# A row load three stores forward in SyncE's order, and three of eight buckets' records loaded from GpSimd's queue

## The chip, the cores and the metric

The kernel runs on one core of a Trainium2 chip. Five engines work side by side, each on its own instruction queue: TensorE (PE; its weight loads are PEld), VectorE (DVE), ScalarE (ACT), GpSimd (POOL) and SyncE (SP), which here issues DMAs and nothing else. GpSimd issues DMAs too. The metric is the device time of one launch in microseconds, the median of several runs.

## What is computed

Block-causal attention (blocks of 64) over 8 batches, 8 heads, 576 positions and head size 64 gives a matrix x of 4608 tokens by 512; a noisy top-2 router then sends each token through two of eight experts:

```python
scores = np.where(mask, scale * np.matmul(q, k.transpose(0, 1, 3, 2)), -1000000000.0)
attn = np.exp(scores - np.max(scores, axis=-1, keepdims=True))
attn = attn / (np.sum(attn, axis=-1, keepdims=True) + 1e-09)
x = np.matmul(attn, v)                                  # as (4608, 512)
noisy_logits = x @ w_gate + np.log1p(np.exp(x @ w_noise)) * noise
top2 = np.argpartition(-noisy_logits, 2, axis=1)[:, :2]
...
h = np.maximum(x[mask] @ w1[e], 0.0)                    # 512 -> 1024
out[mask] += top2_w[mask, k, None] * (h @ w2[e])        # 1024 -> 512
```

## The kernel before

**Stages.** Attention runs first, in four groups of two batches; each group is routed as soon as it is done. GpSimd scatters every token's row of x, with a record of 16 bytes (its two row numbers, a weight, the token's number), into a table in HBM (`xd`, one per half of the tokens). The table has eight buckets of 640 rows per half, one per expert. From about 125 us on TensorE works through 16 buckets in order: 0 to 7 are the first half's experts 0 to 7, 8 to 15 the second half's. A bucket is 640 rows through the expert's two layers: layer 1 (L1017) in two pieces of 320 rows by eight steps, each followed by a relu on ScalarE (L1023), then layer 2 (L1033) in five tiles of 128 rows.

**What a bucket needs.** Its rows: `load_x` (L934), one transposing DMA of 640 rows by 512 from `xd`, issued by SyncE into one of three buffers that take turns (`xg0`, `xg1` and `xT`); in the planner's table it is `LX5.0`, `LX6.0` and so on. Its weights: `load_w` (L910 for layer 1, L912 for layer 2), four DMAs of 512 KB that GpSimd issues and that convert from float32 to bfloat16. They land in memory that attention has left: bucket 5's in `vt`, bucket 6's in `qT` and `kT`, bucket 7's in `esc`.

**What a bucket leaves.** For the first half ScalarE copies each layer-2 tile out (`keep_row`, L1042, `Y.b.c` for tile c of bucket b) into one of ten buffers that take turns: `y0` to `y3`, `zero` and five tiles of `xr0`. SyncE then stores the tile to `yd` in HBM (`store_row`, L1049, `YS.b.c`, 128 KB). A buffer can be written again when its store has landed, ten tiles later: `Y.5.2`, `Y.5.3` and `Y.5.4` go where `Y.3.2`, `Y.3.3` and `Y.3.4` were. GpSimd later gathers rows from `yd` (L1056); VectorE adds and ScalarE scales them (L1040, L1069, L1091), and the sums are stored or scattered (L1075, L1103).

**The records.** `load_rec` (L973 to L976) reads the second half's records, 16 bytes each, into `rc`; `read_rec` (L984 to L1000) makes of them on VectorE the weights and row numbers that bucket 8 and all after it use.

**What sets the order.** A planner (`Plan`) simulates the engines with made-up costs and gives each step a due time; of the steps that could run on a free engine it takes the one due first. The order that comes out of it is fixed in the program: nothing is decided on the chip. `due` is thus a number that sorts, in the planner's time, not in the chip's. The row loads of buckets 2 to 15 are due 12 us ahead of the bucket:

```python
pl.add(f"LX{b}.0", {"SP": 0.3}, lambda x, b=b: load_x(b),
       deps=rows_of([2 * half, 2 * half + 1]), due=d0 - 12., take=[("xg", ("xg", b))],
       dma=2.5, packet=22, hold=True, seq="xg")
```

SyncE's DMAs take eight counters (`DMAHW0` to `DMAHW7`) in turn, so each DMA first waits until the eighth one before it has landed; GpSimd's do the same with `DMASW0` to `DMASW7`.

Of the kernel before, what the change touches and what calls it, by code (L numbers as in the profile page):

```python
# [11 lines left out]
I32 = mybir.dt.int32  # L12
# [200 lines left out]
def kernel(  # L213
# [12 lines left out]
    nc = tc.nc  # L226

    B, H, S, D = q.shape
    N, Dm = out.shape
    E = moe_w_gate.shape[1]  # L230
    F = moe_w1.shape[2]
    assert Dm == H * D and N == B * S
    P = 128
# [7 lines left out]
    CAP = 640  # L241
# [4 lines left out]
    OVB = E * CAP  # L246
    XR = OVB + 2 * TH * P
    DR = Dm + 8
# [12 lines left out]
    xd = [nc.dram_tensor(f"xd{i}", (XR, DR), BF16, kind="Internal").ap() for i in range(NH)]  # L261
# [58 lines left out]
    rc = low.tile([P, E, CT, 4], I32, name="rc")  # L320
# [91 lines left out]
    for g in range(NG):  # L412
        for ch in (4, 0, 1, 2, 3):
            for nm in "qk":
                pl.add(f"L{nm}{g}.{ch}", {"POOL": 0.58 if ch == 4 else 0.74}, lambda e, g=g, nm=nm, ch=ch: load_qk(g, nm, ch),
                       due=due_u(g, first_u[ch]) - (18.,18.,18.,22.)[g] + (0.1 if nm == "k" else 0) - (3 if ch == 4 else 0),
                       take=[("r" + nm, ("raw", g, nm, ch))], dma=0.7 if ch == 4 else 1.41, packet=88)
        for i in range(6):
            pl.add(f"V{g}.{i}", {"POOL": 1.18 if i < 4 else 0.7}, lambda e, g=g, i=i: load_v(g, i),
                   due=due_u(g, 6) - (8. if g else 16.) + i * 0.2, rel=0.0 if g < 1 else due_u(g, 0) - 8.,  # L420
                   take=[("vt", ("vt", g))] if i == 0 else [], deps=[f"V{g}.0"] if i else [],
# [55 lines left out]
    for g in range(NG):  # L477
        for nm in "qk":
            for ch in ("4B", 0, 1, 2, 3, "4A"):
# [4 lines left out]
                else:  # L484
                    need, u, lh = [f"L{nm}{g}.{ch}"], first_u[ch], last_h[ch]
                due = due_u(g, u) - 4 + (0.1 if nm == "k" else 0)
# [4 lines left out]
                       take=[("bk", ("tp", g, nm, ch), 1 if g else 0)], free=fr, lat=0.25)  # L491
# [4 lines left out]
                if ch == 0:  # L496
                    pl.add(f"CW{nm}{g}", {"DVE": 0.12}, lambda e, g=g, nm=nm: wrap(g, nm, e),
                           deps=[f"T{nm}{g}.0"] + ([s_name(g - 1, 7)] if g else []), due=due + 0.6, lat=0.15)
                pl.add(f"C{nm}{g}.{ch}", on,
                       lambda e, g=g, nm=nm, ch=ch: turned(g, nm, ch, e), deps=[f"T{nm}{g}.{ch}"] + prev,  # L500
                       due=due + 0.5, free=[("tp", g, nm, ch)], lat=0.15)
# [460 lines left out]
    def rows_of(gs):  # L962
        return [f"D{g}.{j}" for g in gs for j in range(2 * TG)]

    def rows_landed(ins, half, gs):
        own = [i for g in gs for i in scat[g]]
        apart(ins, f"scat{half}", own)
        for i in own:
            tc.add_manual_dep(ins.ins, i.name, SYNC_DEP, reason="rows landed")
        member(ins, f"rows{half}")  # L970
        return ins

    def load_rec():  # L973
        ins = nc.sync.dma_start(out=rc.rearrange("p e c w -> p (e c) w"),
                                in_=xd[1].bitcast(I32)[0:OVB, Dm // 2:DR // 2].rearrange("(c p) w -> p c w", p=P))
        return rows_landed(ins, 1, [2, 3])  # L976

    def read_rec():
        f = [rc[:, :, :, i].bitcast(I32 if i == 3 else F32) for i in range(4)]
# [130 lines left out]
    for b, i in ORDER:  # L1110
# [3 lines left out]
        if b < EARLY:  # L1114
            for c in range(c0 // P, (c0 + n) // P):
                pl.add(f"LX{b}.{c}", {"SP": 0.4}, lambda x, b=b, c=c: load_tile(b, c),
                       deps=rows_of(groups(b, c // 2)), due=d0 - 8 + c * 0.2, take=[("y", ("xl", b, c))], dma=0.4, packet=47)
                pl.add(f"XT{b}.{c}", {"PE": 0.23}, lambda x, b=b, c=c: turn_tile(b, c), mode="128*128", deps=[f"LX{b}.{c}"],
                       due=d0 - 3, take=[("bk", ("xp", b, c), 1)], free=[("xl", b, c)], lat=0.25)
                pl.add(f"XX{b}.{c}", {"DVE": 0.36, "ACT": 0.6}, lambda x, b=b, c=c: tile_turned(b, c, x),  # L1120
                       deps=[f"XT{b}.{c}"], due=d0 - 2, free=[("xp", b, c)], lat=0.2,
                       take=[("xg", ("xg", b))] if c == 0 else [])
                if c:
                    pl.ops[f"XX{b}.{c}"].deps.append(f"XX{b}.0")
        elif i == 0:
            pl.add(f"LX{b}.0", {"SP": 0.3}, lambda x, b=b: load_x(b),
                   deps=rows_of([2 * half, 2 * half + 1]), due=d0 - 12., take=[("xg", ("xg", b))],
                   dma=2.5, packet=22, hold=True, seq="xg")
        for st in range(FB // nb):
            d1 = d0 + st * nb * 0.55 * n / NW  # L1130
# [320 lines left out]
```

## Time and profile before

| | |
|---|---|
| median of 3 runs | 459.71 us (459.61 to 460.6) |
| the profiled execution | 462.31 us |
| its span, first to last instruction | 460.5 us |
| TensorE busy | 400.1 us (87%) |
| ScalarE busy | 256.0 us (56%) |
| GpSimd busy | 260.1 us (56%) |
| VectorE busy | 162.8 us (35%) |
| DMA queue q0, GpSimd's | 69856 packets, 52.37 MB, 67.3% of 16 engines' span |
| DMA queue q1, SyncE's | 58160 packets, 27.14 MB, 28.3% |

Busy times overlap; their sum says nothing. What counts is where TensorE, the busiest, stands still, and what it then waits for. The profile splits the span into 40 slices of 11.5 us and shows each engine's busy tenths in them; its waits name, for each idle stretch, what ended it; its timeline lists instructions with the time they start, how long they take and, in brackets, how long the engine was idle before them. A SyncE row is an issue: how long SyncE was held by it, not how long the transfer took.

### The profile page before, as it was taken

The page shows a single profiled execution, that of the slowest core. Times are in us where ns is not written, and L with a number is a line of the kernel's source. Part 1 is how long each engine was busy: PE and PEld are TensorE (multiplying, and loading weights), DVE is VectorE, ACT ScalarE, POOL GpSimd, SP SyncE. Part 2 cuts the span into 40 slices and gives each one's busy share as a digit, 9 for nine tenths or more (in the row PEclk, how much of TensorE's full clock was granted, in tenths as well). Part 3 has the DMA queues.
Part 4 walks back from the last instruction along what each step waited for, and adds up shares of the span by engine and source line. Part 5 has one row for each costly group of instructions (what it writes and reads, how often), then busy time and mean ns, then how long its engine had stood idle before and what let it go on. Part 6 is the DMA issues. An engine that isn't in the chain of part 4 may idle for free. (4 is left out here: it accounts for less than half of the span.)

```text
span 460.5 us, 10885 instructions
## 1 busy us (share of the span) xinstructions
PE 400.1 (87%) x4384; PEld 255.7 (56%) x4384; DVE 162.8 (35%) x451; ACT 256.0 (56%) x447; POOL 260.1 (56%) x293
## 2 busy tenths in 40 slices
PE   3899779869697999999899499999998998999950
PEld 3667666657456776555555165565554554655620
DVE  3768698877617510000000020023322423332320
ACT  2898687957791544745554154555554554655410
POOL 8756447877785775672120002433757777777760
PEclk9999999998999999999999799999999999999995
DMA  8999993999999799999999995758688477555430
GB/s 126 189 218 199 193 187 107 130 204 182 233 163 248 172 217 210 276 236 153 193 220 168 215 154 133 133 128 207 115 172 180 139 182 184 181 176 172 146 129 1
DMA packets 128073, 80.26 MB, mean 174 GB/s; under 512 B 85696, under 2 KB 115981, under 8 KB 128016
## 3 DMA queue, kind: packets, MB, share of 16 engines
q0 software_dynamic: 69856, 52.37, 67.3%
q1 hardware_dynamic: 58160, 27.14, 28.3%
q8 instruction: 36, 0.59, 0.5%
q14 instruction: 21, 0.17, 0.1%
HBM read 72.74 MB, written 35.17 MB: 234 GB/s over the span
## 5 line engine op out<-in xcount | busy, mean ns | idle before, releaser
L551 ACT ACTIVATE esc<-sc 128x1024 bf16<-128x1024 f32 x96 | 92.9, 1028 | 20.5 <-PE sc L532 20.0
L1033 PEld LDWEIGHTS <-h 128*128 128x128 bf16 x640 | 62.2, 98 | 72.7 <-issue 7.6
L790 POOL DMA_INDIRECT xd<-xr,slots x72 | 72.0, 1001 | 37.6 <-issue 17.3
L1023 ACT ACTIVATE h<-sc 128x320 bf16<-128x320 f32 (+1 forms) x120 | 49.6, 444 | 47.2 <-PE sc L1017 30.4
L1056 POOL DMA_INDIRECT xr<-yd,slots x36 | 36.8, 1021 | 66.5 <-DMA yd<-zero 44.8
L1023 ACT ACTIVATE h<-bk 128x320 bf16<-128x320 f32 (+1 forms) x124 | 55.7, 456 | 17.2 <-PE bk L1017 12.6
L1017 PEld LDWEIGHTS <-w 128*128 128x128 bf16 x448 | 40.8, 98 | 15.6 <-issue 1.3
L1017 PEld LDWEIGHTS <-esc 128*128 128x128 bf16 x384 | 37.5, 98 | 20.4 <-issue 3.1
L1056 POOL DMA_INDIRECT xr<-yd,grow x35 | 36.4, 1040 | 17.1 <-issue 9.8
L525 PE MATMUL sc<-qT,kT 64*128 64x512 bf16 (+4 forms) x320 | 37.9, 303 | 4.6 <-ACT esc L551 4.1
L984 DVE TENSOR_TENSOR rtmp<-rc,rowid 128x40 f32<-128x40 f32 x1 | 0.2, 226 | 99.1 <-DMA rc<-xd 99.1
L1033 PE MATMUL sc<-esc,h 128*128 128x512 bf16 x136 | 32.0, 379 | 2.2 <-DVE xr L1069 2.0
L1033 PE MATMUL bk<-w,h 128*128 128x512 bf16 x128 | 31.6, 379 | 0.8 <-DVE xr L1069 0.8
L600 PEld LDWEIGHTS <-esc 128*128 128x128 bf16 x640 | 23.9, 99 | 12.9 <-issue 11.0
L600 PE MATMUL bk<-vt,esc 128*128 128x65 bf16 x540 | 24.4, 197 | 4.3 <-DVE xr L622 1.4
L1033 PE MATMUL sc<-w,h 128*128 128x512 bf16 x112 | 27.6, 379 | 0.2 <-ACT h L1023 0.2
L1075 POOL DMA_INDIRECT out_dram<-xr,trow x21 | 21.4, 1019 | 10.0 <-issue 4.6
L460 DVE COPY kT<-bk 128x1024 bf16<-128x1024 bf16 (+1 forms) x24 | 24.9, 1041 | 5.8 <-PE bk L439 5.1
L1017 PE MATMUL sc<-xg,esc 128*128 128x320 bf16 x168 | 26.6, 299 | 0.4 <-ACT h L1023 0.3
L622 DVE TENSOR_TENSOR xr<-bk,rden 128x256 bf16<-128x256 f32 x61 | 25.9, 424 | 2.1
L1033 PE MATMUL bk<-esc,h 128*128 128x512 bf16 x104 | 24.9, 379 | 1.5 <-DMA esc<-in_moe_w_dram 1.5
L1017 PE MATMUL bk<-xg,esc 128*128 128x320 bf16 x152 | 24.4, 299 | 0.0
(212 smaller groups left out, 640.0 us busy)
## 6 DMA issues: line engine op xcount, KB each, us to landing
w<-in_moe_w_dram POOLq DMA_DIRECT2D x12, 512.0 KB
esc<-in_moe_w_dram POOLq DMA_DIRECT2D x12, 512.0 KB
yd<-xr SPq DMA_DIRECT2D x35, 128.0 KB
rq<-in_q_dram POOLq DMA_DIRECT2D x16, 256.0 KB
rk<-in_k_dram POOLq DMA_DIRECT2D x16, 256.0 KB
vt<-in_v_dram POOLq DMA_DIRECT2D x16, 256.0 KB
yd<-y SPq DMA_DIRECT2D x31, 128.0 KB
out_dram<-o SPq DMA_DIRECT2D x24, 128.0 KB
```

The costliest lines, as they stand in the source:

```text
L460: nc.vector.tensor_copy(o, i)
L525: nc.tensor.matmul(out=sc[:, hf, off:off + z - a], lhsT=kT[sl, c0 + jt * P:c0 + jt * P + P], rhs=qT[sl, c0 + a:c0 + z], start=True, stop=n ...
L551: return nc.scalar.activation(out=esc_t[i][:, hh, :, piece * 512:(piece + 1) * 512], in_=sc, func=AF.Exp, scale=scale)
L600: nc.tensor.matmul(out=a[:, hh, :], lhsT=esc[:, hh, hf, c:c + P], rhs=vb[:, jt, hf, h, 0:D + 1], start=(jt == 0), stop=(jt == ib))
L622: nc.vector.tensor_tensor(out=xr[:, idx, st * SET * D:(st + 1) * SET * D].rearrange("p (h d) -> p h d", h=SET), in0=a[:, :, 0:D], in1=rden ...
L790: ins = nc.gpsimd.indirect_dma_start(out=xd[half].bitcast(I32), out_offset=bass.IndirectOffsetOnAxis(ap=slots[:, g * TG + idx, i:i + 1], a ...
L984: vec.tensor_tensor(out=first, in0=f[0], in1=rowid, op=ALU.is_equal)
L1017: nc.tensor.matmul(out=hp[:, j * n:(j + 1) * n], lhsT=w1sb[:, db, fb * P:(fb + 1) * P], rhs=xg[:, db, c0:c0 + n], start=(db == 0), stop=(d ...
L1023: return nc.scalar.activation(out=h_t[pl.slot(("h", b))][:, s * nb:(s + 1) * nb, c0:c0 + n], in_=bank(("hp", b, i, s))[:, 0:nb * n].rearra ...
L1033: nc.tensor.matmul(out=yp, lhsT=h[:, fb, c * P:(c + 1) * P], rhs=w2sb[:, fb, :], start=(fb == 0), stop=(fb == FB - 1))
L1056: ins = nc.gpsimd.indirect_dma_start(out=g_t[pl.slot(key)], out_offset=None, in_=yd[half][0:len(es) * CAP, :], in_offset=bass.IndirectOffs ...
L1075: ins = nc.gpsimd.indirect_dma_start(out=out, out_offset=bass.IndirectOffsetOnAxis(ap=trow[:, e, c:c + 1], axis=0), in_=out_tile(("o", b, ...
```

## The change

Two edits. The row load of bucket 6 (the seventh) gets a due time 44 us ahead of its bucket instead of 12, which moves it in SyncE's order. And the records are loaded by two DMAs: those of the second half's buckets for experts 0 to 2 from GpSimd's queue, those for experts 3 to 7 from SyncE's, as all were before.

```diff
--- before.py
+++ after.py
@@ -971,9 +971,13 @@
         return ins
 
     def load_rec():
-        ins = nc.sync.dma_start(out=rc.rearrange("p e c w -> p (e c) w"),
-                                in_=xd[1].bitcast(I32)[0:OVB, Dm // 2:DR // 2].rearrange("(c p) w -> p c w", p=P))
-        return rows_landed(ins, 1, [2, 3])
+
+        q = 3
+        for eng, e0, e1 in ((nc.gpsimd, 0, q), (nc.sync, q, E)):
+            ins = eng.dma_start(out=rc[:, e0:e1].rearrange("p e c w -> p (e c) w"),
+                                in_=xd[1].bitcast(I32)[e0 * CAP:e1 * CAP, Dm // 2:DR // 2].rearrange("(c p) w -> p c w", p=P))
+            rows_landed(ins, 1, [2, 3])
+        return ins
 
     def read_rec():
         f = [rc[:, :, :, i].bitcast(I32 if i == 3 else F32) for i in range(4)]
@@ -1124,7 +1128,7 @@
                     pl.ops[f"XX{b}.{c}"].deps.append(f"XX{b}.0")
         elif i == 0:
             pl.add(f"LX{b}.0", {"SP": 0.3}, lambda x, b=b: load_x(b),
-                   deps=rows_of([2 * half, 2 * half + 1]), due=d0 - 12., take=[("xg", ("xg", b))],
+                   deps=rows_of([2 * half, 2 * half + 1]), due=d0 - (44. if b == 6 else 12.), take=[("xg", ("xg", b))],
                    dma=2.5, packet=22, hold=True, seq="xg")
         for st in range(FB // nb):
             d1 = d0 + st * nb * 0.55 * n / NW
```

Nothing else changes on any engine: TensorE's, ScalarE's and VectorE's orders are the same, the operations too. In the changed file the lines behind L973 stand four further down (L1049 is L1053, L1056 is L1060).

On SyncE, around the row load of bucket 6 (`xg0_110`, from `xd0`); `y0` to `y3`, `zero` and `xr0` are the tiles' buffers, `rc` the records, `xg1_111` bucket 7's rows. Before:

```order
L1049 DMA yd0<-y0_114 128x512
L1049 DMA yd0<-y1_115 128x512
L1049 DMA yd0<-y2_116 128x512
L1049 DMA yd0<-xr0_107 128x512 x2
L934 DMA_TRANSPOSE xg0_110<-xd0 128x4x640
L1049 DMA yd0<-xr0_107 128x512 x3
L1049 DMA yd0<-y3_117 128x512
L1049 DMA yd0<-zero_160 128x512
L1049 DMA yd0<-y0_114 128x512
L1049 DMA yd0<-y1_115 128x512
L974 DMA rc_122<-xd1 128x40x4
L934 DMA_TRANSPOSE xg1_111<-xd0 128x4x640
```

Now:

```order
L1053 DMA yd0<-y0_114 128x512
L1053 DMA yd0<-y1_115 128x512
L934 DMA_TRANSPOSE xg0_110<-xd0 128x4x640
L1053 DMA yd0<-y2_116 128x512
L1053 DMA yd0<-xr0_107 128x512 x5
L1053 DMA yd0<-y3_117 128x512
L1053 DMA yd0<-zero_160 128x512
L1053 DMA yd0<-y0_114 128x512
L1053 DMA yd0<-y1_115 128x512
L977 DMA rc_122<-xd1 128x25x4
L934 DMA_TRANSPOSE xg1_111<-xd0 128x4x640
```

The load stands ahead of the three stores `YS.3.2` to `YS.3.4` (`y2` and two of `xr0`), which were ahead of it; the rest keeps its order.

The same place with what each waits for (`DMAHWn` is the landing of the eighth DMA before it). Before, from the row load of bucket 6 on:

```order
L934 DMA_TRANSPOSE xg0_110<-xd0 128x4x640 [waits DMAHW4_49,PE_49]
L1049 DMA yd0<-xr0_107 128x512 [waits DMAHW5_49,Activation_49]
L1049 DMA yd0<-xr0_107 128x512 [waits DMAHW6_49,Activation_49]
L1049 DMA yd0<-xr0_107 128x512 [waits DMAHW7_49,Activation_49]
L1049 DMA yd0<-y3_117 128x512 [waits DMAHW0_49,Activation_49]
L1049 DMA yd0<-zero_160 128x512 [waits DMAHW1_49,Activation_49]
L1049 DMA yd0<-y0_114 128x512 [waits DMAHW2_49,Activation_49]
L1049 DMA yd0<-y1_115 128x512 [waits DMAHW3_49,Activation_49]
L974 DMA rc_122<-xd1 128x40x4 [waits DMASW5_49,DMASW4_49,DMASW6_49,DMASW3_49,DMASW7_49,DMASW2_49,DMAHW4_49,DMASW1_49,DMASW0_49]
L934 DMA_TRANSPOSE xg1_111<-xd0 128x4x640 [waits DMAHW5_49,PE_49]
```

Now, from the first of the three moved stores on:

```order
L1053 DMA yd0<-y2_116 128x512 [waits DMAHW2_49,Activation_49]
L1053 DMA yd0<-xr0_107 128x512 [waits DMAHW3_49,Activation_49]
L1053 DMA yd0<-xr0_107 128x512 [waits DMAHW4_49,Activation_49]
L1053 DMA yd0<-xr0_107 128x512 [waits DMAHW5_49,Activation_49]
L1053 DMA yd0<-xr0_107 128x512 [waits DMAHW6_49,Activation_49]
L1053 DMA yd0<-xr0_107 128x512 [waits DMAHW7_49,Activation_49]
L1053 DMA yd0<-y3_117 128x512 [waits DMAHW0_49,Activation_49]
L1053 DMA yd0<-zero_160 128x512 [waits DMAHW1_49,Activation_49]
L1053 DMA yd0<-y0_114 128x512 [waits DMAHW2_49,Activation_49]
L1053 DMA yd0<-y1_115 128x512 [waits DMAHW3_49,Activation_49]
L977 DMA rc_122<-xd1 128x25x4 [waits DMASW5_49,DMASW4_49,DMASW6_49,DMASW3_49,DMASW7_49,DMASW2_49,DMAHW4_49,DMASW1_49,DMASW0_49]
L934 DMA_TRANSPOSE xg1_111<-xd0 128x4x640 [waits DMAHW5_49,PE_49]
```

The row load now takes counter 1 and not 4. So the store of `zero` waits for the row load's landing, the next two stores and the record load wait for the three moved stores, and bucket 7's row load waits for the same store as before (the first `xr0` behind the moved ones, counter 5).

On GpSimd, between its last weight loads and its first gathers. Before:

```order
L912 DMA kT_149<-in_moe_w2_dram 128x4x512 x2
L910 DMA esc0_140<-in_moe_w1_dram 128x2x1024 x2
L912 DMA esc1_141<-in_moe_w2_dram 128x4x512 x2
L1056 DMA xr0_107<-yd0,slots_101 128x512 x4
L1056 DMA xr1_108<-yd0,slots_101 128x512 x5
```

Now:

```order
L912 DMA kT_149<-in_moe_w2_dram 128x4x512 x2
L910 DMA esc0_140<-in_moe_w1_dram 128x2x1024 x2
L912 DMA esc1_141<-in_moe_w2_dram 128x4x512 x2
L977 DMA rc_122<-xd1 128x15x4
L1060 DMA xr0_107<-yd0,slots_101 128x512 x4
L1060 DMA xr1_108<-yd0,slots_101 128x512 x5
```

One DMA is added, behind the last weight load of bucket 7 and ahead of the first gather.

## Rows read from the trace of the kernel before

**Rows 1.** The page's slices of the span: TensorE's busy tenths and granted clock.

```profile
PE   3899779869697999999899499999998998999950
PEclk9999999998999999999999799999999999999995
```

**Rows 2.** Waits of all engines, 195 to 262 us: us in total, times, longest.

```profile
PE sc L1017 <- DMA xg<-xd: 6.8, 1, 6.8
```

**Rows 3.** TensorE's timeline, 249 to 281 us: start, us, instruction; idle before, its releaser.

```profile
252.75 1.03 PE L1033 MATMUL sc<-vt,h 128*128 128x512 bf16 x4
260.54 1.23 PE L1017 MATMUL sc<-xg,qT 128*128 128x320 bf16 x4 [6.77 <-DMA xg<-xd]
267.59 3.62 PE L1033 MATMUL sc<-kT,h 128*128 128x512 bf16 x16
280.06 0.71 PE L1017 MATMUL bk<-xg,esc 128*128 128x320 bf16 x4
```

**Rows 4.** SyncE's timeline, 185 to 300 us: its DMA issues.

```profile
198.92 14.28 SPq L934 DMA_TRANSPOSE xT<-xd  x1
213.73 0.32 SPq L1049 DMA_DIRECT2D yd<-xr  x1
229.32 13.14 SPq L934 DMA_TRANSPOSE xg<-xd  x1
260.59 0.40 SPq L974 DMA_DIRECT2D rc<-xd  x1
261.73 8.39 SPq L934 DMA_TRANSPOSE xg<-xd  x1
```

**Rows 5.** SyncE's timeline in short windows: single stores.

```profile
218.65 1.29 SPq L1049 DMA_DIRECT2D yd<-y  x1
227.81 0.32 SPq L1049 DMA_DIRECT2D yd<-xr  x1
242.56 5.73 SPq L1049 DMA_DIRECT2D yd<-xr  x1
```

**Rows 6.** SyncE's waits in windows 213 to 229, 226 to 232, 254 to 262 us.

```profile
SPq L1049 <- DMA xT<-xd: 7.0, 1, 7.0
SPq L934 <- DMA yd<-xr: 1.1, 1, 1.1
SPq L974 <- DMA xg<-xd: 5.5, 1, 5.5
SPq L934 <- DMA yd<-xr: 0.7, 1, 0.7
```

**Rows 7.** Stretches: busy us of PE, PEld, DVE, ACT, POOL; clock, DMA share, GB/s.

```profile
270.00:275.00 5.00, 4.81 (x33) 3.06 (x32) 1.87 (x12) 3.34 (x7) 0.00 (x0) 1.00 1.10 248
253.50:256.90 3.40, 0.27 (x2) 0.00 (x0) 0.00 (x0) 0.09 (x1) 0.00 (x0) 1.00 1.17 192
256.90:263.70 6.80, 3.16 (x10) 1.47 (x10) 0.00 (x0) 0.13 (x1) 0.00 (x0) 0.50 1.22 225
```

**Rows 8.** ScalarE's timeline, 249 to 264.5 us.

```profile
252.13 0.60 ACT L1042 ACTIVATE y<-bk 128x512 bf16<-128x512 f32 x1 [2.14 <-PE bk L1033]
263.57 0.44 ACT L1023 ACTIVATE h<-sc 128x320 bf16<-128x320 f32 x1 [9.98 <-PE sc L1033]
263.91 0.59 ACT L1042 ACTIVATE xr<-sc 128x512 bf16<-128x512 f32 x1
```

**Rows 9.** GpSimd's timeline, 185 to 300 us; then one source line (ns min/median/max).

```profile
284.86 1.07 POOL L1056 DMA_INDIRECT xr<-yd,slots  x1 [44.77 <-DMA yd<-zero]
...
L397 POOL DMA_DIRECT2D vt<-in_v_dram x16: 1140/1180/1269, 5.6 to 130.2; - x16
```

**Rows 10.** Timelines of VectorE and ScalarE: who reads the records first.

```profile
269.12 0.23 DVE L984 TENSOR_TENSOR rtmp<-rc,rowid 128x40 f32<-128x40 f32 x1 [99.12 <-DMA rc<-xd]
...
306.93 1.27 ACT L1040 ACTIVATE xr<-sc,wrow 128x512 bf16<-128x512 f32 x2 [2.89 <-issue]
```

**Rows 11.** TensorE's waits from 265 us to the end.

```profile
PE sc L1033 <- DVE xr L1069: 2.0, 1, 2.0
```

## The prediction

> **What bounds the kernel now.** I read the slices of the span first. TensorE is busy in eight tenths or more of every slice from the fourteenth on but one: the slice from 253 to 265 us has a 4, and the granted clock its 7 [rows 1]. So the end of the kernel is TensorE's work plus its holes, and the question is what this hole is. The waits of that stretch give it one cause: 6.8 us, once, for the landing of `xg<-xd` [rows 2]. TensorE's timeline gives the place: layer 2 of bucket 5 from 252.75, then nothing until 260.54, where layer 1 of bucket 6 (weights in `qT`) starts on the transposing load of its rows [rows 3]. From 265 us to the end TensorE's longest wait is 2.0 us, for VectorE [rows 11], so what is gained at 260 us should still be there at the end.
>
> Then SyncE, which issues that load. It begins the load at 229.32 and is held for 13.14 us, so the rows land 31 us after the issue begins [rows 3, 4]. What takes so long? The bucket-5 load ahead of it was issued at 198.92 [rows 4]; a store at 227.81 waited 7.0 us for it to land [rows 5, 6]. The next in line, the store issued at 213.73, landed at 229.3, which is what the bucket-6 load waited for last, 1.1 us [rows 4, 6]. A store of 128 KB that is 15 us under way and lands just behind the load ahead of it has stood in a line: SyncE's transfers are served about in the order of their issue, while GpSimd's weight loads use the same DMA engines. So the bucket-6 load did not start moving at 229.32; it stood behind eight stores that had been issued or were due before it. What counts is not when it is issued but how many transfers stand ahead of it.
>
> **The change, part by part.**
>
> *Three stores fewer ahead of the load.* The load now takes the place of the store at 218.65 [rows 5], and bucket 3's last three stores (`YS.3.2` to `YS.3.4`) stand behind it. At 218.65 the load ahead is still in flight, so the new load waits in line; it wins those three stores' service time and no more. The trace has this time twice. Behind the bucket-5 load the next store landed at 229.3 against 227.8: 1.5 us. Behind the bucket-6 load the record load's wait ends at 260.5, and the bucket-7 load, which waits for the next store's landing, starts at 261.73 [rows 4, 6]: 1.2 us. Three stores are 3.6 to 4.5 us. Below, the price can be bounded by a stretch without weight loads: 248 GB/s [rows 7] would carry 3 x 131 KB in 1.6 us. I take 1.2 us each, since that row was measured where this load lands, under the same traffic: **3.6 us**. The load lands near 256.9 instead of 260.5, and TensorE's hole shrinks from 6.8 to 3.2 us.
>
> *TensorE's clock.* It is granted in full to 256.9, 3.1 us after the hole began, and at half (1.2 of 2.4 GHz) from 256.9 to 263.7 [rows 7]. TensorE works in the last 3.2 us of that, which costs 1.6 us. With a hole of 3.2 us the fall comes just as work starts again; I take the same loss as now, so **0**, with a gain of 1.6 as the other end.
>
> *The three stores behind the load.* They free the buffers that ScalarE fills next: the outputs `Y.5.2` to `Y.5.4`, whose first is written at 252.13 today [rows 8]. With the load landing at 256.9 and 1.2 us per store, the buffers come free at 258.1, 259.3 and 260.5. ScalarE, in order, then writes 258.1 to 258.7 and 259.3 to 259.9, and is free for bucket 6's first relu at 259.9. Today that relu runs 3.03 us after TensorE's first matmul, at 263.57 [rows 3, 8], since it is released with the layer-2 piece behind it; 256.9 + 3.0 is also 259.9. The third write would be due at 260.3 (3.37 us after the first matmul, as now) and finds its buffer at 260.5. TensorE needs the accumulator of that write only for layer 2, 7.0 us after its start [rows 3]. So **0**; if the clock does not fall, TensorE comes 1.5 us sooner to the relu and I give back up to 0.4.
>
> *The line behind.* A DMA of SyncE waits for the landing of the eighth before it. Today that makes the record load wait 5.5 us for the bucket-6 load [rows 6]. Afterwards the store of `zero` waits for that load, the next two and the record load for the three moved stores, and the bucket-7 load for the same store as today: four stores after 256.9, that is 261.7, against 261.73 now [rows 4]. Nothing behind is later. But bucket 7 now begins 3.6 us sooner, at 276.5 instead of 280.06 [rows 3]. SyncE is through with issuing its load at 270.1 [rows 4], and 655 KB at 248 GB/s [rows 7] are another 2.6 us: an estimate of 273 us for the landing, 3.5 us to spare. **0**; the other end is that up to 3.6 us is given back there.
>
> *Records of buckets 0 to 2 from GpSimd's queue.* GpSimd issues one DMA more, behind the last weight load; its nearest kind in size of piece is the load of `v`, 1.18 us an issue, and its queue stands idle 44.77 us before 284.86 [rows 9]: **0**. The waits of this DMA are for scatters long landed. SyncE's record load shrinks from 40 to 25 pieces per partition, which can only bring the bucket-7 load forward, into time it does not need. VectorE reads the records at 269.12 and ScalarE multiplies by them first at 306.93 [rows 10], so even 10 us of delay of one half is covered. If that cover were gone, ScalarE's first output of bucket 8 would wait us for us.
>
> **Sum.** 0 + 0 + 0 + 0 - 3.6 against the profiled execution's 462.31 us (span 460.5) gives 458.7. That execution is 2.6 us over the median of the shown runs, 459.71; on the median the forecast is **456.1 us**.
>
> **The rivals.**
>
> *The stores cost less than they seem.* If the 1.2 to 1.5 us are mostly the weight loads' share, which moves on anyway, the load wins only the stores' own bytes: 1.6 us, so 458.1. For it speaks the shared traffic; against it, that the weight loads stay in line at every place that the load can take. The Trainium skill, "DMA: Bandwidth & Descriptors", Specifications, gives the fabric a ceiling of 435 GB/s; by it three such stores take 0.9 us, and the sum would be 458.8. The trace, with 1.2 and 1.5 us a store, does not bear that out.
>
> *The place in line does not count.* If a transposing load starts only when the one before it is done and its own issue is through, nothing is won: 459.7. Against it: the store issued just behind the bucket-5 load was served 1.5 us behind it, so the line does not pause at a transposing load.
>
> *The landing follows the issue.* If transfers share rather than stand in line, the load lands 10.7 us sooner, the whole hole goes, and the clock with it: 6.8 + 1.6 = 8.4 us, 451.3. Against it speaks the store of 213.73.
>
> *The clock stays up.* The hole is 3.2 us and the fall came 3.1 us into it; a little less, and TensorE restarts at 2.4 GHz: 3.6 + 1.6 - 0.4 = 4.8, so 454.9. The Trainium skill, "TensorE: Matmul & The Clock Gate", Part 1, says the gate is set by how busy TensorE has been recently; by it a halved hole may leave the clock up, and the sum would be the 454.9 just worked out.
>
> *Slower: ScalarE stands before its buffers.* The three stores behind the load may land far later than 1.2 us apart: one store's issue alone held SyncE 5.73 us in this stretch [rows 5]. If the third lands at time T, its output is written by T + 0.6, three relus take 1.4, and layer 2 starts 0.2 later, at T + 2.2, against 267.59 today [rows 3]. The point is T = 265.4; beyond it the kernel is slower than before. At 4 us a store T is 268.9, and the kernel takes 459.7 + 3.5 = 463.2.
>
> **Chances.** Forecast 0.57; clock stays up 0.12; landing follows issue 0.07; stores cost less 0.08; place does not count 0.10; ScalarE's buffers 0.06. The bounds of the forecast's own terms (4.5 us of stores and 1.6 of clock) reach down to 453.6. Upward the range takes in cheap stores and no effect, 459.8. It leaves out the full gain and the slower case, 0.13. About 0.2% (0.9 us) is what a measurement of this kernel can tell from no change. Faster by more: forecast, clock, full gain and cheap stores hold 0.84; less 0.04 for a forecast that falls short, 0.80. Within: the case without effect and most of those 0.04, 0.13. Slower: 0.07.
>
> **What the changed profile would show.** The load issued near 218.7; TensorE's wait for `xg<-xd` near 3.2 us instead of 6.8; ScalarE's writes `Y.5.2` and on delayed from 252 to about 258 with a DMA (`yd`) named as releaser; the bucket-7 load still issued near 261.7 and no new wait at bucket 7's start; GpSimd's first gather earlier by the same 3.6 us; the gap between 265 us and the end unchanged. The prediction is wrong if the wait stays near 6.8, if it vanishes, if TensorE waits again at bucket 7, or if the wait goes and the end does not move.

## The result and the profile after

The changed kernel takes 448.64 us (median of 6 runs, 444.82 to 453.4); the kernel before took 460.51 us beside it (6 runs, 459.61 to 462.27). The ratio is 0.9719, 95% interval 0.9653 to 0.9785: 11.9 us less, where 3.6 were forecast and the range ended at 453.6. The direction was right, the size was not. (The ratios here and below are of the runs in the chip's faster state alone, the medians are of all runs, so the two can differ by some tenths of a per cent.)

The profiled execution took 450.79 us, 2.2 us over its median (that of the kernel before was 1.8 over its own); its span is 449.0, 11.5 us under the span before. First the stretch that the prediction spoke of. The waits of the changed kernel (releaser after the arrow; sum, count, longest in us):

```profile
ACT y L1046 <- DMA yd<-y: 5.6, 1, 5.6
...
PE sc L1021 <- ACT h L1027: 2.4, 4, 2.0
...
PE sc L1021 <- DMA xg<-xd: 0.6, 1, 0.6
```

The wait for the row load of bucket 6 is 0.6 us instead of 6.8 [rows 2], and TensorE has a wait for ScalarE of 2.0 us, where before the longest such wait was 0.2. TensorE's timeline shows where both are:

```profile
255.47 0.70 PE L1021 MATMUL sc<-xg,qT 128*128 128x320 bf16 x4 [0.58 <-DMA xg<-xd]
...
260.09 0.70 PE L1021 MATMUL sc<-xg,qT 128*128 128x320 bf16 x4 [1.97 <-ACT h L1027]
...
275.27 0.57 PE L1021 MATMUL bk<-xg,esc 128*128 128x320 bf16 x3
```

Bucket 6 begins at 255.47 instead of 260.54, bucket 7 at 275.27 instead of 280.06 and without a wait [rows 3]. SyncE's timeline:

```profile
216.92 24.79 SPq L934 DMA_TRANSPOSE xg<-xd  x1
...
259.11 0.40 SPq L977 DMA_DIRECT2D rc<-xd  x1
260.29 8.82 SPq L934 DMA_TRANSPOSE xg<-xd  x1
```

The load is issued 12.4 us sooner than in [rows 4], lands 5 us sooner, and holds SyncE for 24.79 us instead of 13.14. Not all of that is the edit's. By the landings that the traces record, the load of bucket 5, which is ahead of it in both kernels, happened to land 2.6 us sooner in this execution (225.13 against 227.75); from that landing to the one of bucket 6's load it is 30.3 us instead of 32.8. TensorE also came to bucket 6 by 1.1 us later (254.89 against 253.77, the starts of bucket 6 less the idle time before them). So of the 6.2 us by which the wait shrank, 2.5 belong to the load's new place, and 3.7 are luck of this pair: with the load in either place, bucket 5's load lands anywhere from 224 to 229 us and TensorE arrives anywhere from 250 to 255 in the profiles of the first, second and fourth group.

ScalarE, in its timeline, pays for the new place with a wait for the store that now stands behind the load:

```profile
250.66 0.44 ACT L1027 ACTIVATE h<-bk 128x320 bf16<-128x320 f32 x1
256.67 0.60 ACT L1046 ACTIVATE y<-bk 128x512 bf16<-128x512 f32 x1 [5.57 <-DMA yd<-y]
258.21 0.60 ACT L1046 ACTIVATE xr<-bk 128x512 bf16<-128x512 f32 x1 [0.94 <-PE bk L1021]
```

And the clock: of the two stretches of [rows 7] behind TensorE's hole, the second had 0.50. By stretch, the changed kernel (columns: stretch, length, busy time and count of PE, PEld, DVE, ACT, POOL, then granted clock, DMA share, GB/s):

```profile
253.50:256.90 3.40, 2.81 (x16) 1.32 (x15) 0.00 (x0) 0.23 (x1) 0.00 (x0) 1.00 1.16 229
256.90:263.70 6.80, 4.83 (x34) 3.13 (x33) 0.00 (x0) 4.28 (x10) 0.00 (x0) 1.00 1.18 242
```

What was gained up to there shows in the last scatter of GpSimd, the last DMA of the program: it is issued 4.4 us sooner. In the timelines of GpSimd, before and after:

```profile
445.68 0.98 POOL L1075 DMA_INDIRECT out_dram<-xr,trow  x1 [0.31 <-issue]
```

```profile
441.26 0.98 POOL L1079 DMA_INDIRECT out_dram<-xr,trow  x1 [0.30 <-issue]
```

From there to the end of the span it is 14.8 us before (460.5 - 445.7) and 7.8 us after (449.0 - 441.3). **The other 7.1 of the 11.5 us come from behind the last useful instruction.** The two instructions that hold them are on GpSimd's sequencer, at the program's closing lines (L1362 and L1446 before; four lines further down after). They are not counted as busy and stand in no list of the costliest groups. The view of these lines gives shortest, median and longest duration in ns. Before:

```profile
L1362 POOLq INC_SWDGE_SEM  x1: 2230/2230/2230, 449.0 to 449.0; - x1
...
L1446 POOLq DRAIN  x3: 51/103/8398, 451.3 to 460.2; - x3
```

After:

```profile
L1366 POOLq INC_SWDGE_SEM  x1: 870/870/870, 444.4 to 444.4; - x1
...
L1450 POOLq DRAIN  x3: 51/103/2845, 445.3 to 448.7; - x3
```

DRAIN went from 8.398 to 2.845 us and the semaphore step ahead of it from 2.230 to 0.870: 6.9 us. No engine does work of the program during the DRAIN: by the trace's semaphores, all engines wait at the closing line for one that GpSimd's sequencer sets behind it (at 459.8 us before, 448.3 after). SyncE's waits there show the length, before and after; the releaser that the view names, TensorE's sequencer (PEq), stands at the same line and waits too:

```profile
SPq L1446 <- PEq L1446: 8.4, 2, 7.9
```

```profile
SPq L1450 <- PEq L1450: 2.8, 2, 2.3
```

### The profile page after: what moved, and what is told of

Read it like the earlier page. It is cut to its first block, busy times and chain, and to the rows that moved or that the text cites. A ratio compares the mean times of both kernels' runs of the same rounds, so it can differ in the third digit from the quotient of the medians.

```text
span 449.0 us, 10885 instructions
## 1 busy us (share of the span) xinstructions
PE 405.8 (90%) x4384; PEld 259.0 (58%) x4384; DVE 162.9 (36%) x451; ACT 256.2 (57%) x447; POOL 262.5 (58%) x294
## 4 chain that ended last, share of the span: by engine, by line
PE 45%; POOL 18%; DMA 17%; issue 11%; DVE 5%; ACT 2%; POOLq 0%; ACTq 0%; DVEq 0%
PE sc L1037 9%; DMA xg<-xd 9%; PE sc L1021 8%; PE bk L1021 8%; PE bk L1037 8%; POOL xr L1060 7%; POOL out_dram L1079 5%; POOL xd L790 4%; DMA vt<-in_v_dram 4%; PE sc L525 3%; PE bk L439 2%; PE bk L600 2%; DMA rk<-in_k_dram 2%; DVE xr L622 1%; DMA rq<-in_q_dram 1%
## 5 line engine op out<-in xcount | busy, mean ns | idle before, releaser
L1060 POOL DMA_INDIRECT xr<-yd,slots x36 | 37.3, 1037 | 57.0 <-DMA yd<-zero 38.3
L1060 POOL DMA_INDIRECT xr<-yd,grow x35 | 36.5, 1044 | 18.1 <-issue 10.4
L525 PE MATMUL sc<-qT,kT 64*128 64x512 bf16 (+4 forms) x320 | 40.7, 321 | 3.4 <-ACT esc L551 3.1
L532 PE MATMUL sc<-ones_mat,maskA 64*128 64x64 bf16 x256 | 24.1, 201 | 2.2 <-issue 2.2
```

Of the source, the lines that this page charges most:

```text
L525: nc.tensor.matmul(out=sc[:, hf, off:off + z - a], lhsT=kT[sl, c0 + jt * P:c0 + jt * P + P], rhs=qT[sl, c0 + a:c0 + z], start=True, stop=n ...
L532: nc.tensor.matmul(out=sc[:, hf, off:off + 64], lhsT=maskA[sl, :], rhs=ones_mat[sl, 0:64], start=False, stop=True, skip_group_check=True)
L1060: ins = nc.gpsimd.indirect_dma_start(out=g_t[pl.slot(key)], out_offset=None, in_=yd[half][0:len(es) * CAP, :], in_offset=bass.IndirectOffs ...
```

## The experiments

Eighteen runs were made in five groups, of fifteen new kernels (two of them twice) and of the changed one again, each beside the kernel before on the same chip. Executions of one kernel spread over 3 to 17 us (8 to 27 in group 3) for reasons that no run isolates, so medians of 4 to 12 runs do not tell two us apart; the closing instructions repeat to the nanosecond and tell much more. "Step" is INC_SWDGE_SEM; n is explained under the table; the wait is TensorE's for the row load of bucket 6. The filler is a load of 7 x 128 pieces that nobody reads.

| kernel | wait, us | step, us | DRAIN, us | n | median, us | ratio to before, 95% |
|---|---|---|---|---|---|---|
| before | 6.8 | 2.230 | 8.398 | 102 | | |
| changed | 0.6 | 0.870 | 2.845 | 34 | 448.64 | 0.9719 (0.9653 to 0.9785) |
| changed again | 4.6 | 0.870 | 2.845 | 34 | 449.12 | 0.9833 (0.9788 to 0.9878) |
| load forward only | 5.6 | 2.230 | 8.398 | 102 | 456.04 | 0.9926 (0.9878 to 0.9975) |
| split only | 6.1 | 0.870 | 2.845 | 34 | 451.43 | 0.982 (0.977 to 0.9871) |
| one small load more | 4.6 | 2.250 | 8.480 | 103 | 460.7 | 1.006 (1.0019 to 1.0102) |
| spare pieces | 7.0 | 0.870 | 2.845 | 34 | 450.89 | 0.9742 (0.9644 to 0.984) |
| 1 bucket (5 row tiles) | 4.6 | 2.330 | 8.807 | 107 | 460.28 | 0.9878 (0.9749 to 1.0008) |
| 2 buckets (10) | 1.9 | 0.600 | 1.702 | 20 | 445.29 | 0.9672 (0.9583 to 0.976) |
| all 8 buckets (40) | 4.5 | 1.310 | 4.642 | 56 | 453.73 | 0.9801 (0.9673 to 0.9929) |
| 7 row tiles | 2.0 | 0.460 | 1.130 | 13 | 450.11 | 0.9724 (0.9627 to 0.982) |
| 7 tiles, load not forward | 6.1 | 0.460 | 1.130 | 13 | 450.8 | 0.9805 (0.9741 to 0.9869) |
| 7 tiles, load further | none | 0.460 | 1.130 | 13 | 453.69 | 0.9889 (0.982 to 0.9958) |
| filler at 22 us | 7.2 | 2.230 | 8.398 | 102 | 459.1 | 0.9976 (0.9941 to 1.001) |
| seven small loads | | 2.370 | 8.970 | 109 | | |
| filler at 198 us | | 0.380 | 0.803 | 9 | | |

All DRAINs lie within 1 ns on 0.068 us + n x 0.08167 us with a whole number n (counted so that the rest is less than one step); the step before it is 0.20 us + n x 0.02 us within 0.01. Both therefore follow the same count, n, and together cost 0.102 us for each.

**Group 1: the parts.** The changed kernel again, each edit alone, and one small GpSimd load added to the kernel before. The load forward only:

```diff
-                   ... due=d0 - 12., ...
+                   ... due=d0 - (44. if b == 6 else 12.), ...
```

> Only the row load of bucket 6 stands three stores further forward; all records are loaded by SyncE, and GpSimd issues no DMA more. In the changed kernel's trace the last scatter of GpSimd starts 4.4 us sooner (441.26 against 445.68), but the span is 11.5 us shorter; the rest lies behind the last scatter, where GpSimd's DRAIN takes 2.8 us instead of 8.4 and its INC_SWDGE_SEM 0.9 instead of 2.2. Theory A: the end got shorter because GpSimd issues one DMA more, so here the DRAIN stays near 8.4 and the time falls by the load's part alone, 4 to 5.5 us, to about 455.5. Rival B: the end got shorter because the kernel's work ends sooner or otherwise, so here the DRAIN is near 2.8 and the time near 449. In both TensorE's wait for the load of bucket 6 falls from 6.8 to below 2 us, and ScalarE waits some 5 us for a store's buffer at the second output of bucket 5's last three.

The split only is the changed kernel with this line back as it was.

> Only the records are split: three buckets from GpSimd's queue; the row load of bucket 6 stands where it stood. Theory A (one GpSimd DMA more shortens the end): TensorE's wait for bucket 6's rows stays near 6.8 us, the last scatter starts near 445.7, the DRAIN takes about 2.8 us, and the time falls by 5.5 to 7 us, to about 454. Rival B: the DRAIN stays near 8.4 and the time is that of the kernel before, 460, within 1 us.

The small load (128 pieces of 64 bytes that nobody reads):

```diff
     def load_rec():
+        nc.gpsimd.dma_start(out=spare, in_=moe_w_gate.rearrange("(p b) e -> p b e", p=P))
```

> The kernel before, with one small DMA more on GpSimd's queue at the place of the split's (the gate's weights, 32 numbers per partition, into a tile that nobody reads; 128 x 32 values); the records stay with SyncE. If theory A holds for any DMA more: DRAIN about 2.8 us, time about 454. If it is the many small pieces of the split's DMA that count (1920 of 16 bytes), or the shorter SyncE record load: DRAIN 8.4, time 460.

> The changed kernel once more, for a second profile: its six runs spread from 444.8 to 453.4 us where those of the kernel before spread from 459.6 to 462.3. If the end behind the last scatter is what spreads, the profile shows another DRAIN length, and the time from the first instruction to the last scatter is 441 to 442 us as before; if the body spreads, the last scatter moves with the time and the DRAIN is again about 2.8 us. Median expected 448.6 within 3 us.

On this chip the kernel before had a median of 458.0 us. The load forward only took 2.0 us off that, the split only 6.6, both 8.9 (11.9 on the first chip; the intervals of the two ratios do not meet). By the medians the two edits add up. By the ratios the split only and both are not told apart (0.982 and 0.9833), so the times leave open what the load adds to the split. Either way the larger share is that of the edit that the prediction put at nothing. The load forward only missed one expectation: TensorE's wait fell to 5.6 us, not below 2. The changed kernel again has its last scatter at 439.4 us and the same DRAIN: what spreads is the work, not the end. The closing lines say where the split's share lies. Load forward only, split only, and one load more:

```profile
L1446 POOLq DRAIN  x3: 51/103/8398, 445.0 to 454.0; - x3
```

```profile
L1450 POOLq DRAIN  x3: 51/103/2845, 447.5 to 450.9; - x3
```

```profile
L1449 POOLq DRAIN  x3: 51/103/8480, 441.7 to 450.8; - x3
```

The long end goes with the records undivided, wherever the load stands and whenever the end comes (445.0 against 451.3 us before, and the same 8398 ns). It is not chance from run to run. One more load on GpSimd does not shorten it; it makes it 82 ns longer.

**Group 2: is it what SyncE loses or what GpSimd gets?** The spare pieces copy the split's GpSimd load into a tile that nobody reads and leave SyncE all eight buckets:

```diff
-        ins = nc.sync.dma_start(out=rc..., in_=xd[1]...[0:OVB, ...])
-        return rows_landed(ins, 1, [2, 3])
+        for eng, dst, e1 in ((nc.gpsimd, spare, 3), (nc.sync, rc, E)):
+            ins = eng.dma_start(out=dst..., in_=xd[1]...[0:e1 * CAP, ...])
+            rows_landed(ins, 1, [2, 3])
+        return ins
```

> The kernel before, with one GpSimd load more: the same 1920 pieces of 16 bytes that the split moves, at the place that the split gives them, but into a tile that nobody reads; SyncE still loads all the records itself, and the seventh bucket's load stays where it was. Theory (what GpSimd's last DRAIN costs depends on how much has been put on GpSimd's own queue, whatever it was for): DRAIN 2.845 us and the semaphore step before it 0.870 us, as in the changed kernel and in the split alone; time some 7 us under the kernel before. Rival (SyncE's queue, relieved of 30 KB in small pieces, is what makes the end shorter): DRAIN 8.4 us or longer, 2.23 us for the step, time within 2 us of the kernel before.

The others are the changed kernel with one line each:

```diff
-        q = 3
+        q = 1
```

> The changed kernel with the records of one bucket on GpSimd instead of three: 40 pieces for each of the 16 DMA engines instead of 120. The small load of the run with the spare load had 8 pieces and one closing write on each DMA engine and made DRAIN 0.082 us longer, some 9 ns an entry. Theory (a count on GpSimd's queue that starts over somewhere between 9 and 121 entries more than before): DRAIN either 8.40 + 41 x 0.009 = 8.77 us (not yet started over; then the time is that of the forward load alone, 2 to 3 us under before) or 2.85 - 80 x 0.009 = 2.1 us (started over; then 0.7 us under the changed kernel). Rival (in proportion to what SyncE no longer loads): one third of the 5.55 us, DRAIN 6.5 us, time between the two kernels.

with `q = 2`:

> The changed kernel with the records of two buckets on GpSimd. Theory of the count that starts over: DRAIN either 8.40 + 81 x 0.009 = 9.14 us or 2.85 - 40 x 0.009 = 2.48 us, and nothing between. Rival (in proportion to what SyncE no longer loads): two thirds of the 5.55 us, DRAIN 4.7 us.

and with `q = E` and no load from SyncE:

> The changed kernel with the records of all eight buckets on GpSimd, none on SyncE. Theory of the count: 200 entries more than in the changed kernel, DRAIN 2.85 + 200 x 0.009 = 4.7 us, the end 1.8 + 0.45 us later, time 2 us over the changed kernel. Rival (relief of SyncE): DRAIN at or under 2.85 us, time at or under the changed kernel's.

The spare pieces and the one bucket, at the closing line:

```profile
L1450 POOLq DRAIN  x3: 51/103/2845, 450.0 to 453.3; - x3
```

```profile
L1450 POOLq DRAIN  x3: 51/103/8807, 451.3 to 460.7; - x3
```

The spare load does all of it, to the nanosecond, while SyncE does what it always did: relief of SyncE is out. So is a proportion to what is moved, since one bucket makes the end longer (8.807, where the count gave 8.77 and the proportion 6.5). All eight give 4.642, as the count had it (4.7). Two buckets give 1.702 instead of 2.48: the end did fall below that of three buckets, but further than 40 entries are worth. A count that starts over fits one bucket and eight, and misses two.

**Group 3** ran on a chip with a granted clock of 0.91 to 0.92 in all profiles, where every execution took over 510 us (the kernel before 531.62); its times spread too far to tell the kernels apart, its closing lines do not. Two buckets with the load not forward, once more, and with the load three stores further:

```diff
-                   ... due=d0 - (44. if b == 6 else 12.), ...
+                   ... due=d0 - 12., ...
```

> Two buckets' records on GpSimd, as in the run before with two, but the seventh bucket's load back in its old place behind the three stores; GpSimd's instructions are word for word those of that run. Theory: the end of the kernel hangs on GpSimd's queue alone, so DRAIN is 1.702 us again, and the time differs from the same kernel with the load forward by the load's own worth: 2 to 3.5 us longer. Rival (the place of the load in line is worth nothing, the gain was all at the end): within 1 us of it.

> Two buckets' records on GpSimd and the load forward, once more, as the partner of the two others of this group. DRAIN 1.702 us, time 445 to 447 us, 1.5 us under the changed kernel.

```diff
-                   ... due=d0 - (44. if b == 6 else 12.), ...
+                   ... due=d0 - (52. if b == 6 else 12.), ...
```

> The same with the load three more stores forward: six stores of the old order now go behind it. If each store passed is worth 1.2 us until the wait is gone, the 2 to 5 us of TensorE's wait that are left for this load go to nothing; what takes its place is the wait of ScalarE for the buffers of the stores now behind the load (5.6 to 10 us of ScalarE in the runs with the load forward, of which TensorE felt 0 to 2.4 us), which starts earlier. Theory: no net gain, within 1.5 us of the partner; TensorE's wait for the load under 1 us, its waits for ScalarE 3 us or more. Rival (the load's place is what bounds): 2 to 4 us under the partner.

Seven row tiles on GpSimd (a bucket has five):

```diff
-        q = 3
-        for eng, e0, e1 in ((nc.gpsimd, 0, q), (nc.sync, q, E)):
+        q, cat = 7, rc.rearrange("p e c w -> p (e c) w")
+        for eng, e0, e1 in ((nc.gpsimd, 0, q), (nc.sync, q, E * CT)):
+            ins = eng.dma_start(out=cat[:, e0:e1], in_=xd[1]...[e0 * P:e1 * P, ...])
```

> The changed kernel with seven row tiles' records (7 x 128 pieces of 16 bytes, 56 pieces and one closing write on each DMA engine) on GpSimd, the other 33 on SyncE: between the 41 entries that did not start the count over and the 81 that did. Theory of the count: DRAIN either 8.40 + 57 x 0.010 = 8.97 us, time about that of the run with one bucket, or started over and shorter than with two buckets, 1.70 - 24 x 0.010 = 1.46 us, and then the shortest end of all. Anything between 2 and 8.4 us speaks against the count.

The times: 526.09, 523.46, 537.11 and 528.76 us, each spread over 8 to 27 us. The ratio of the seven tiles to the kernel before is 1.0035 there (0.9951 to 1.0118): the 9.0 us by which its closing lines are shorter do not show in that time. The two kernels that differ only by the load's place are 2.6 us apart by median, as expected, but far less than they spread. The DRAIN of the first three was 1702 ns each time, although it begins some 80 us later than in group 2; of the seven tiles:

```profile
L1450 POOLq DRAIN  x3: 51/103/1130, 529.9 to 531.5; - x3
```

The seven tiles' 1.130 us is under both values that were expected (8.97 and 1.46). The length belongs to the program and not to its timing: a chip that needs 77 us more for the two buckets gives the same DRAIN.

**Group 4: the load's place with the same end, and the place of the entries.** Seven tiles with the load forward, not forward, and three stores further (edits as in group 3):

> The changed kernel with seven row tiles' records on GpSimd, again. DRAIN 1.130 us and the step before it 0.460 us as in the first run of it; the end is 8.398 + 2.230 - 1.130 - 0.460 = 9.0 us shorter than before's, and 2.1 us shorter than the changed kernel's. Time 2 us under the changed kernel, 11 to 13 us under the kernel before.

> The same with the seventh bucket's load back in its old place. DRAIN 1.130 us. Theory (the load's place is worth what the prediction said or a little less): 2 to 3.6 us over its partner with the load forward. Rival (the place is worth nothing): within 1 us.

> The same with the load three stores further forward still. DRAIN 1.130 us. Theory (TensorE's wait passes from the load to ScalarE, which waits for the buffers of the stores now behind the load): TensorE's wait for the load under 1 us, its waits for ScalarE 3 us or more, time within 1.5 us of the partner. Rival (the load's place is what bounds): 2 to 4 us under the partner.

The filler is seven tiles' worth of pieces at 22 us in the kernel before:

```diff
     def load_wgn():
+        nc.gpsimd.dma_start(out=spare, in_=moe_noise[0:7 * P, 0:4].rearrange("(c p) w -> p c w", p=P))
         nc.gpsimd.dma_start(out=wgn[:, 0], ...)
```

> The kernel before with one GpSimd load more, at 22 us, of 7 x 128 pieces of 16 bytes into a tile that nobody reads; load and records stay as they were. Theory (the number of entries on GpSimd's queue is all that counts): DRAIN 1.130 us and 0.460 us for the step before it, as with seven tiles of the records at 240 us; 9.0 us of the end gone, 0.7 us of GpSimd's time added early where it is seldom waited for: 8 to 9.5 us under the kernel before. Rival (the entries have to come where the split puts them): DRAIN 8.97 us, time that of the kernel before or 0.5 us over it.

The load's place is worth 0.7 us of median here (450.11 against 450.8), 2.0 and 2.3 in group 1; by the ratios it is 0.8% (3.7 us) here, 0.7% (3.4 us) for the load alone and nothing on top of the split. Of these differences in time only that of the load alone against the kernel before is clear of the noise. Going further costs 3.6 us of median (453.69), where at most 1.5 had been expected, and TensorE's timeline in that kernel names what takes over:

```profile
251.99 2.31 PE L1037 MATMUL bk<-vt,h 128*128 128x512 bf16 x5 [10.84 <-ACT h L1027]
```

with ScalarE's reason in its own timeline:

```profile
251.01 0.60 ACT L1046 ACTIVATE zero<-sc 128x512 bf16<-128x512 f32 x1 [12.12 <-DMA yd<-zero]
```

TensorE no longer waits for the load but 10.8 us for ScalarE, which waits for a store that now stands behind the load. The filler at 22 us left the end exactly as it was:

```profile
L1449 POOLq DRAIN  x3: 51/103/8398, 448.1 to 457.1; - x3
```

It hit neither expectation (1.130 or 8.97): this load, put on the queue that early, does not count at the end at all.

**Group 5**, again on a chip with a granted clock of 0.91 to 0.92 (the kernel before 539.35 us; the two kernels 533.41 and 533.37, medians that do not show the 10.2 us between their closing lines). Seven small loads at the split's place, and the filler at the fifth expert's weights:

```diff
     def load_rec():
+        for i in range(7):
+            nc.gpsimd.dma_start(out=spare[:, i], in_=moe_w_gate.rearrange("(p b) e -> p b e", p=P))
```

> The kernel before with seven small GpSimd loads at the split's place, each of the kind that made 102 steps 103 (8 KB into a tile that nobody reads). Theory (a whole load of 128 pieces is one step, and the steps go down once they would pass 107 or 108): 102 + 7 = 109 steps are too many, DRAIN as with seven row tiles of records, 13 steps, 1.13 us, or near it, and 8 to 9 us off the end. Rival (the pieces of 16 bytes matter, or the load's bytes): 109 steps, DRAIN 0.068 + 109 x 0.0817 = 8.97 us, no gain.

```diff
     def load_w(e, which, part):
+        if (e, which, part) == (4, 1, 0):
+            nc.gpsimd.dma_start(out=spare, in_=moe_noise[0:7 * P, 0:4].rearrange("(c p) w -> p c w", p=P))
```

> The kernel before with the filler of 7 x 128 pieces of 16 bytes at 198 us, ahead of the fifth expert's weights. If an entry counts wherever GpSimd has not started over since: DRAIN 1.13 us and 9 us off the end. If GpSimd starts over between 198 and 232 us: DRAIN 8.398 us unchanged, time that of the kernel before. Neither of the two is favoured.

```profile
L1450 POOLq DRAIN  x3: 51/103/8970, 521.7 to 531.2; - x3
```

```profile
L1450 POOLq DRAIN  x3: 51/103/803, 532.9 to 534.2; - x3
```

The seven loads came out as the rival had it: 109 steps, 8.970 us where 8.97 was expected. My limit of 107 or 108 steps falls. The filler, which did nothing at 22 us, at the fifth expert's weights (245.7 us in this execution) gives the shortest end of all, 0.803 us and 9 steps, not the 13 that the same number of pieces gives at the split's place.

**What is shown and what is open.** Shown: GpSimd's two closing instructions together take 0.27 us + 0.102 us for each of n steps; n is fixed by the program; it depends on the loads on GpSimd's own queue, not on SyncE's, not on who reads what is loaded, and not on the time. A small load at the split's place adds one step; five row tiles in one load add five; seven or more in one load take 46 to 89 away. Open: what sets n. A plain count of entries with a limit does not do it, since seven loads of 8 pieces for each DMA engine add seven steps where one load of 56 pieces for each takes 89 away, and since the place in the program decides. It may be that one long load must fit what is left of some store of entries, and starts that store over if it does not; no run shows that store.

## Why the prediction was wrong

**The bound: right.** TensorE's hole at 254 us was the load's wait; moving the load shrank it, though that it all but vanished in the changed kernel's own profile was luck for the larger part (2.5 of 6.2 us). Over the profiles taken at clocks of 0.966 or more, the wait is 6.8, 6.1, 4.6, 7.0, 6.1 and 7.2 us with the load in its old place (mean 6.3) and 0.6, 4.6, 5.6, 4.6, 1.9, 4.5 and 2.0 in the new one (mean 3.4).

**Three stores at 1.2 us: right in kind, somewhat too large.** The means differ by 2.9 us instead of 3.6, about 1.0 a store. The landings say the same with less spread: in these profiles bucket 6's load lands 30.9 to 33.4 us behind bucket 5's in the old place (mean 31.9) and 27.2 to 30.3 in the new (mean 29.0), 2.8 us less. The last scatter starts at 436.3 to 445.9 us in the old place (mean 442.6) and at 434.9 to 445.1 in the new (mean 439.3), 3.3 us less; the 4.4 of the one pair lie within that spread. The price of one store was right: the six stores behind the load land 1.2 us apart in the mean (255.43 to 262.43), and ScalarE's write behind the first starts at 256.67, 1.2 us after TensorE has the load. The rule that the prediction set against it, the fabric's ceiling in the Trainium skill ("DMA: Bandwidth & Descriptors", Specifications), made it 0.9 us for all three; the measured 2.9 us are not that. The rival that the landing follows the issue falls too: from issue to the start of bucket 6 it was 31.2 us, [rows 3, 4], and is now 38.6 (255.47 - 216.92), so the load stands in line as supposed. Its time of 451.3 was nearer to the result for a reason that did not occur.

**The clock, 0: wrong in the changed kernel's profile, open in others.** The hole was 0.6 us in that execution and the clock stayed at 1.00 (2.4 GHz) where it had been 0.50 (1.2 GHz). In the profiles of the changed kernel again and of the load forward only, with 4.6 and 5.6 us of wait left, it fell again, for 3.4 and 6.8 us. With waits of 1.95 us (two buckets) and 1.96 us (seven row tiles) it stayed up in the first and fell for 3.4 us in the second, so the length of the hole alone does not decide. The Trainium skill ("TensorE: Matmul & The Clock Gate", Part 1) says the gate is set by how busy TensorE has been recently. The changed kernel's profile, in which the hole was shorter than I forecast, agrees with that; for holes of 2 us these two profiles leave open what it would make of them.

**ScalarE's buffers, 0 or 0.4 given back: too small in two profiles of seven.** TensorE gave back 1.97 us at 260.09 in the changed kernel, and 1.74 in the run with two buckets; in the other five profiles with the load in the new place it was 0.3 at most. Bucket 6 began 5.1 us sooner and bucket 7 4.8. The rival that I gave 0.06, ScalarE before its buffers, does not decide here, but it does with three more stores behind the load: 10.8 us of TensorE and 453.69 us against 450.11.

**The line behind, 0: right.** Bucket 7's load is issued at 260.29 against 261.73, and bucket 7 does not wait.

**The records on GpSimd's queue, 0: the step that failed.** "GpSimd issues one DMA more" was priced at its issue and at who waits for its data; that part held (1.22 us of issue in an idle queue, no wait at bucket 8). But the same load changes what GpSimd has to close at the end, by 68 steps of 0.102 us: **6.9 us**, nearly twice the one term that the sum consisted of. The spare pieces show that it is this load and not SyncE's relief, the load forward only that it is not the row load's place. The sentence that "what is gained at 260 us should still be there at the end" held for the work (185.1 us from bucket 6 to the last scatter before, 445.68 - 260.54, and 185.8 after, 441.26 - 255.47), and the one that the gap from 265 us to the end stays unchanged failed for what comes behind it. Measured in the two profiles, 4.4 us up to the last scatter and 7.1 us behind it make the 11.5 us of the spans. Over all profiles it is about 3 us for the load's place and 6.9 for the end, 10 us, between the 8.9 and the 11.9 us that the medians fell by. Why n falls from 102 to 34 stays open.

Could it have been seen? That the end was long, yes: the prediction read TensorE in [rows 1] as busy "in eight tenths or more of every slice from the fourteenth on but one", but that row ends in a 5 and a 0; 14.8 us lie between the last scatter and the end of the span before, and the closing lines name DRAIN with 8.398 us. So the end of the kernel was not only TensorE's work and its holes. That the split would shorten it, no row of before tells; the price of the end should have stood in the sum as an unknown, from all of DRAIN's 8.4 us gained to as much lost, and the range should have reached further down.

**A better version.** Two buckets or seven row tiles instead of three end 1.4 and 2.1 us sooner by the closing lines. In time they took 0.9672 (0.9583 to 0.976) and 0.9724 (0.9627 to 0.982) of the kernel before; both beat that one, and neither is shown to be faster than the changed kernel (0.9719 beside the first result, 0.9833 on the second chip). The best single load found for the end alone, the filler at the fifth expert's weights, was not tried together with the load forward.

## What to carry to other kernels

Read the profile to its last microsecond: subtract the last useful instruction's time from the span, and look up what the sequencers do in between, since those instructions count as busy nowhere. Whoever moves or adds a load on GpSimd's queue may change that end too (here one load at 22 us did not, those from 198 us on did), and a measured gain may lie there and have nothing to do with the purpose of the move; take each part alone before believing the reason. A load moved ahead of stores in a queue gains their service time only until the buffers that those stores free become what the next engine waits for.

## What the runs showed of the hardware

GpSimd's closing DRAIN took 0.803 to 8.970 us in programs that do the same work, always 0.068 us and a whole multiple of 0.08167 us, and the same to the nanosecond in executions of one program that differ by 77 and 91 us in length (two buckets, seven tiles). An 8 KB load that nobody needs can lengthen the end by 0.1 us, and a 14 KB one shorten it by 9.4 us (2.230 + 8.398 before, 0.380 + 0.803 with the filler at the fifth expert's weights). Around bucket 6 the transfers of SyncE's queue landed in the order of their issue: in the changed kernel's profile the five stores ahead of the load landed at 227.74 to 232.69 us, the load at 255.43, the six stores behind it at 256.56 to 262.43; and 12.4 us of earlier issue shortened its distance to the load ahead by 2.5 us.
